# Attention and two MoE layers on one core: four small edits to buffers, banks and the place of one subtraction

## The chip, the cores and the metric

The program runs on one core of one Trainium2 chip. The metric is device time in microseconds (us) of one execution, as the median of several. Engines are named as in the profile: PE (TensorE, matmuls), DVE (VectorE), ACT (ScalarE), POOL (GpSimd), SP (SyncE, which only issues transfers here).

## The reference, cut to what matters

```
# 32 heads (4 batches x 8), 576 positions, head width 64, blocks of 64
scores = q @ k.T / 8, masked where block(query) < block(key)
attn   = exp(scores - max) / (sum + 1e-9)
x      = attn @ v                       # heads side by side: 2304 x 512
h1     = max(x @ w_in1, 0);   x2 = h1*h1 @ w_out1
h      = x2 @ w_in2                     # 2304 x 2048
P      = a0 + a1*h + a2*h^2 + a3*h^3;   Q = 1 + |b0||h| + |b1|h^2
out    = P / (Q + 1e-6) @ w_out2
```

## The kernel before, in words

**Three stages.** Until about 405 us the heads' attention runs, and the first half of the first MoE layer is woven into it (`moe_a`, six blocks of tokens, k = 0 to 5). Until 603 us the second half of that layer runs, and then the second layer, five blocks of tokens by 16 units u (hc, L780, is a unit's first product, yc, L898, its second). A scheduler places every instruction in its engine's queue when the program is built; each engine then runs its queue strictly in order and waits on semaphores. So an edit that adds a dependence, or takes one away, can reorder much that it does not name.

**High and low parts.** From head 10 (PLAIN) on each fp32 operand is split in a high part (float32r) and a remainder, the low part, and products are summed from three or four combinations. For head n, qh and kk are made one head ahead: ACT copies the high parts (L259, L260), DVE writes the low part of q into half of the tile q_two (L263; q_two and k_two exist twice and alternate over the heads), POOL writes the low part of k into the upper half of kk (L265), and SP copies kk's lower half into k_two (L266). PE's score products of head n (L335) read kk whole, so they wait for L265. The constant halves of q_two and k_two are filled once, by L231 and L232 in `make_two`.

**The other names.** p holds exponentials (ACT L371, normalised on POOL L399); tp is p transposed by PE (L300) in PSUM, which ACT (L441, high) and DVE (L443, low) move into pt (before head 10: pt_plain, L429); pv (L483) is p times v. ACT L486 and DVE L487 bring pv into xp, POOL L492 and L493 split xp into ring, the x that MoE reads. A tile of PSUM has a tag, and a tag has a number of banks ("mm" 2, "tp" 3); a product that takes a bank again waits for the readers of what was there. In `moe_a` ha (L540) goes to ACT (relu and square, L575 and L576) and DVE (L578, tile s), and POOL makes the low part (L579).

**The last stage's element work for unit u.** ACT: L878 |h| into ab, L880, L879 into wq; POOL squares (L881); DVE L882, L883 read h for the last time when r is not h's bank; then one unit later ACT Ln (L862) and Exp (L863, into r), DVE L864, L865, L866, all reading r; then ACT L857 and POOL L858 make g, which yc reads. ab has two buffers, h four banks: hc of u+4 needs the bank of u, and ab of u+2 the buffer of u.

Of the kernel before, what the change touches and what calls it, by code (L numbers as in the profile page):

```python
# [11 lines left out]
AF = mybir.ActivationFunctionType  # L12
ALU = mybir.AluOpType
# [4 lines left out]
P = 128  # L18
S = 576
SP = 640  # L20
D = 64
# [8 lines left out]
PLAIN = 10  # L30
# [14 lines left out]
def f(ap):  # L45
    return ap.bitcast(F32)
# [3 lines left out]
def attention_moe_moe(ctx: ExitStack, tc: tile.TileContext, q, k, v, wi1, wo1, wi2, wo2, a, b, out):  # L50
    nc = tc.nc
# [171 lines left out]
    q_two, k_two = [], []  # L223

    def make_two(un):
        early.release()
        late = tc.alloc_tile_pool(name="late", bufs=1, reuse_waits="tile")
        for n in range(2):
            q_two.append(late.tile([P, SP], F32R, name=f"q_two{n}"))
            k_two.append(late.tile([P, S], F32R, name=f"k_two{n}"))  # L230
            nc.scalar.activation(q_two[n][D:P], un.qr[D:P], AF.Copy)  # L231
            nc.scalar.activation(k_two[n][D:P], un.kr[D:P], AF.Copy)  # L232
        return late

    def load_v(un):
        src = v[un.hd].rearrange("p (c d) -> p c d", d=D)
# [12 lines left out]
    def prep_qk(un, step):  # L249
        if un.plain:  # L250
            if step == 0 and un.scale == 1.0:
                cols = un.qr[:, un.q0:un.q1]
                nc.gpsimd.tensor_scalar(cols, cols, SCALE, 0.0, op0=ALU.mult, op1=ALU.add)
            return
        if step == 0:
            hd = un.hd
            un.qh = attn.tile([P, SP], F32R, tag="qh", name=f"qh{hd}", bufs=2)
            un.kk = attn.tile([P, S], F32R, tag="kk", name=f"kk{hd}", bufs=2)
            nc.scalar.activation(un.qh, un.qr, AF.Copy, scale=SCALE)  # L259
            nc.scalar.activation(un.kk, un.kr, AF.Copy)  # L260
        else:
            un.q2, un.k2 = q_two[un.hd % 2], k_two[un.hd % 2]
            nc.vector.scalar_tensor_tensor(  # L263
                un.q2[0:D], un.qr[0:D], SCALE, f(un.qh[0:D]), op0=ALU.mult, op1=ALU.subtract)
            nc.gpsimd.tensor_tensor(un.kk[D:P], un.kr[D:P], f(un.kk[D:P]), op=ALU.subtract)  # L265
            nc.sync.dma_start(f(un.k2[0:D]), f(un.kk[0:D]))  # L266

    def prep_v(un, step):
# [20 lines left out]
    spsum, stats, gates, marks, spread = {}, {}, {}, [], {}  # L289
# [163 lines left out]
    def emit_pv(un, half):  # L453
# [4 lines left out]
        n = end - first  # L458
# [30 lines left out]
        if odd:  # L489
            at = S * (b_ % 2)  # L490
            xh, xl = (ring[:, z, hp, at + first:at + end] for z in range(2))
            nc.gpsimd.tensor_scalar(xh, xp[:, 0:n], 1.0, 0.0, op0=ALU.mult, op1=ALU.add)  # L492
            nc.gpsimd.tensor_tensor(xl, xp[:, 0:n], f(xh), op=ALU.subtract)  # L493
            nc.sync.dma_start(xs[:, hp, S * b_ + first:S * b_ + end], xp[:, 0:n])

    wA = {}
# [25 lines left out]
    def moe_a(k):  # L522
# [5 lines left out]
        def bank(nm):  # L528
            nonlocal count
            count += 1  # L530
            tag = "tp" if end_ and count % 2 else "mm"
            return ps1.tile([P, 512], F32, tag=tag, name=nm, bufs=BANKS[tag])

        gs = []
# [109 lines left out]
    for i in range(NI + 5):  # L644

        if i == FIRST:
            moes += [moe_a(0), moe_a(1)]
        elif i in (SECOND, SECOND + PER_B):
            moes.append(moe_a((i - MOE_AT) // PER_B))
        elif i == NI + 3:  # L650
            moes += [moe_a(4), moe_a(5)]
        if i < NI:
            emit_s(i)
        if 0 < i < 3:
            keep_busy(3, marks[-1])
        if 0 <= i - 1 < NI:
            emit_norm(i - 1)
        if i < NI:
            emit_max(i)
        gate = marks[-1 - AHEAD] if i < NI and i > AHEAD else None  # L660
        advance(steps(i + 0.5) - steps(i), gate)
        if i < NI:
            emit_exp(i)
        if 0 <= i - 4 < NI:
            un, gi = slots[i - 4]
            if gi % 2:
                emit_pv(un, gi // 2)
        if 0 <= i - 3 < NI:
            emit_t(i - 3)
        advance(steps(i + 1) - steps(i + 0.5), gate)  # L670
        if i == 4 * PLAIN - 4:
            late = make_two(slots[i][0])
        for back in range(4):
            n = units_at.get(i - back)
            if n is None:
                continue
            if back < 2 and n + 1 < len(units):
                prep_qk(units[n + 1], back)
                ahead = 4 if n + 4 < 2 * H else 2 if n + 2 >= 2 * H else 0
                if back == 1 and ahead and n + ahead < len(units):  # L680
                    load_qk(units[n + ahead])
            elif back >= 2:
                prep_v(units[n], back - 2)
                if back == 3 and n + 1 < len(units):
                    load_v(units[n + 1])
        if due(i) < due(i + 1):
            convA(*gates.values())
# [161 lines left out]
    for u in range(max(downs) + 1):  # L849
# [19 lines left out]
        if u < len(units):  # L869
# [11 lines left out]
            squared = (nc.vector if u >= len(units) - END else nc.gpsimd).tensor_tensor(w, w, ab, op=ALU.mult)  # L881
            nc.vector.tensor_tensor(t, h, t, op=ALU.mult)  # L882
            done = (taken, nc.vector.scalar_tensor_tensor(t, t, a1, h, op0=ALU.add, op1=ALU.mult))  # L883
            mid[u] = (ab, w, t, ab if u < LAG else h)
            if j + 1 < len(blocks3) and 3 <= m < 3 + 2 * KK and m % 2:
                with tc.issue_after(taken.ins), tc.issue_after(squared.ins):
                    split_x(xt[j + 1], m // 2 - 1, blocks3[j + 1][1])
# [81 lines left out]
```

## Time and profile before

| what | value |
|---|---|
| median of 3 runs | 1005.95 us (1005.1 to 1006.06) |
| the profiled execution | 1004.93 us, of which 1003.2 us span |
| PE busy | 992.0 us of the span |
| DVE, ACT, POOL busy | 724.8, 723.8, 570.5 us |
| mean granted TensorE clock | 1.000 |

PE's busy time is nearly the span, so what counts are the few places where PE waits, and what it waits for; the other engines' idle time counts only where it ends at such a place.

### The profile page before, as it was taken

The page shows a single profiled execution, that of the slowest core. Times are in us where ns is not written, and L with a number is a line of the kernel's source. Part 1 is how long each engine was busy: PE and PEld are TensorE (multiplying, and loading weights), DVE is VectorE, ACT ScalarE, POOL GpSimd, SP SyncE. Part 2 cuts the span into 40 slices and gives each one's busy share as a digit, 9 for nine tenths or more (in the row PEclk, how much of TensorE's full clock was granted, in tenths as well). Part 3 has the DMA queues.
Part 4 walks back from the last instruction along what each step waited for, and adds up shares of the span by engine and source line. Part 5 has one row for each costly group of instructions (what it writes and reads, how often), then busy time and mean ns, then how long its engine had stood idle before and what let it go on. Part 6 is the DMA issues. An engine that isn't in the chain of part 4 may idle for free.

```text
span 1003.2 us, 16323 instructions
## 1 busy us (share of the span) xinstructions
PE 992.0 (99%) x5361; PEld 864.6 (86%) x5361; DVE 724.8 (72%) x1389; ACT 723.8 (72%) x1590; POOL 570.5 (57%) x617
## 2 busy tenths in 40 slices
PE   8999999999999999999999999999999999999998
PEld 6678999888888899999888887888888888899997
DVE  7898687877787478767768766757666666666765
ACT  7888697887886467655455557867777777787885
POOL 5777597886787268421215386854655554555542
PEclk9999999999999999999999999999999999999999
DMA  9864334334332244569654651002001100200000
GB/s 295 267 198 149 114 113 132 89 106 130 105 107 83 97 131 124 207 184 300 230 191 151 231 157 58 1 1 84 1 1 32 42 1 1 74 1 1 32 1 32
DMA packets 63844, 106.67 MB, mean 106 GB/s; under 512 B 17040, under 2 KB 33424, under 8 KB 63760
## 3 DMA queue, kind: packets, MB, share of 16 engines
q1 hardware_dynamic: 63184, 105.05, 33.5%
q8 instruction: 42, 0.69, 0.3%
q10 hardware_dynamic: 576, 0.59, 0.2%
q14 instruction: 42, 0.34, 0.1%
HBM read 79.30 MB, written 23.07 MB: 102 GB/s over the span
## 4 chain that ended last, share of the span: by engine, by line
PE 91%; ACT 3%; DVE 2%; POOL 1%; DMA 1%; issue 1%; POOLq 0%; DVEq 0%; ACTq 0%; SPq 0%
PE yc L898 19%; PE hc L780 19%; PE hb L780 10%; PE yb L821 10%; PE ya L562 10%; PE ha L540 9%; PE tp L300 5%; PE pv L483 4%; PE sx L335 3%; PE sy L335 2%; PE pv L470 1%; DMA qr<-in_q_dram 1%; DMA raw_ai<-in_wi_dram 1%; POOL rb L387 0%; ACT p L371 0%
## 5 line engine op out<-in xcount | busy, mean ns | idle before, releaser
L780 PE MATMUL hc<-ring,w_ci 128*128 128x512 f32 (+1 forms) x960 | 210.2, 368 | 1.0 <-DVE t L866 1.0
L780 PEld LDWEIGHTS hc<-ring,w_ci 128*128 128x128 f32 x960 | 176.2, 188 | 27.0 <-DVE t L866 1.4
L898 PE MATMUL yc<-w_co,gc 128*128 128x512 f32 x792 | 191.7, 390 | 0.0
L898 PEld LDWEIGHTS yc<-w_co,gc 128*128 128x128 f32 x792 | 148.2, 188 | 29.3
L858 POOL TENSOR_TENSOR gc<-t,gc 128x512 fp32r<-128x512 f32 (+1 forms) x70 | 85.1, 1215 | 89.4 <-issue 61.0
L881 POOL TENSOR_TENSOR wq<-wq,ab 128x512 f32<-128x512 f32 (+1 forms) x78 | 92.8, 1190 | 75.0 <-ACT wq L879 74.7
L540 PE MATMUL ha<-ring,w_ai 128*128 128x512 f32 (+3 forms) x576 | 117.5, 348 | 0.5 <-DVE xp L487 0.5
L821 PE MATMUL yb<-gb,w_bo 128*128 128x512 f32 (+1 forms) x480 | 105.3, 367 | 0.0
L780 PE MATMUL hb<-ring,w_bi 128*128 128x512 f32 (+1 forms) x480 | 105.2, 367 | 0.0
L540 PEld LDWEIGHTS ha<-ring,w_ai 128*128 128x128 f32 x576 | 94.1, 189 | 11.3 <-issue 3.0
L715 POOL TENSOR_TENSOR ring<-ring 128x512 fp32r<-128x512 f32 (+1 forms) x40 | 52.4, 1311 | 88.0 <-ACT ring L714 83.2
L882 DVE TENSOR_TENSOR t<-hc,t 128x512 f32<-128x512 f32 (+1 forms) x80 | 50.9, 636 | 67.7 <-ACT t L880 67.7
L821 PEld LDWEIGHTS yb<-gb,w_bo 128*128 128x128 f32 x480 | 87.6, 188 | 11.4
L780 PEld LDWEIGHTS hb<-ring,w_bi 128*128 128x128 f32 x480 | 87.5, 188 | 11.1
L562 PE MATMUL ya<-gring,w_ao 128*128 128x352 f32 (+3 forms) x480 | 88.9, 331 | 0.0
L864 DVE SCALAR_TENSOR_TENSOR wq<-wq,hc 128x512 f32<-128x512 f32 (+1 forms) x78 | 49.3, 632 | 53.0 <-ACT hc L863 35.6
L300 PE MATMUL tp<-ident,p 128*128 128x128 f32 x480 | 82.1, 281 | 1.4 <-DVE stat L394 1.0
L562 PEld LDWEIGHTS ya<-gring,w_ao 128*128 128x128 f32 x480 | 75.9, 188 | 4.0 <-DVE s L578 0.2
L399 POOL TENSOR_SCALAR p<-p,stat 64x64 f32<-64x64 f32 (+4 forms) x110 | 60.3, 552 | 28.9 <-DVE stat L395 14.4
L443 DVE TENSOR_TENSOR pt<-tp,pt 128x128 fp32r<-128x128 f32 (+2 forms) x176 | 63.2, 391 | 18.6 <-ACT pt L441 11.9
L441 ACT ACTIVATE pt<-tp 128x128 fp32r<-128x128 f32 (+2 forms) x176 | 56.7, 365 | 19.3 <-PE tp L300 17.4
L878 ACT ACTIVATE ab<-hc 128x512 f32<-128x512 f32 (+1 forms) x80 | 44.2, 553 | 36.3 <-PE hc L780 36.0
(157 smaller groups left out, 2099.3 us busy)
## 6 DMA issues: line engine op xcount, KB each, us to landing
kr<-in_k_dram SPq DMA_DIRECT2D x32, 288.0 KB, 3.6
raw_ci<-in_wi_dram SPq DMA_DIRECT2D x16, 512.0 KB, 4.4
raw_co<-in_wo_dram SPq DMA_DIRECT2D x16, 512.0 KB, 4.0
qr<-in_q_dram SPq DMA_DIRECT2D x24, 320.0 KB, 3.2
ring<-xs SPq DMA_DIRECT2D x24, 256.0 KB, 4.2
raw_ai<-in_wi_dram SPq DMA_DIRECT2D x8, 512.0 KB, 5.2
raw_ao<-in_wo_dram SPq DMA_DIRECT2D x8, 512.0 KB, 4.6
raw_bi<-in_wi_dram SPq DMA_DIRECT2D x8, 512.0 KB, 3.9
```

Of the source, the lines that this page charges most:

```text
L300: yield nc.tensor.transpose(ps[:, P * n:P * (n + 1)], ptile(un, t)[:, P * c:P * (c + 1)], ident)
L399: nc.gpsimd.tensor_scalar(pv, pv, st[r:P, 6 + n:7 + n], 0.0, op0=ALU.mult, op1=ALU.add)
L441: nc.scalar.activation(high, src, AF.Copy)
L443: nc.vector.tensor_tensor(low, src, f(high), op=ALU.subtract)
L540: nc.tensor.matmul(ps[:, 0:n], w[:, zw, P * kk:P * (kk + 1)], ring[:, zx, kk, x0:x0 + n], start=i == 0, stop=i == 3 * KK - 1)
L562: nc.tensor.matmul(ps[c][:, 0:n], wA["o", m][:, zw, P * c:P * (c + 1)], gs[m][:, zg, 0:n], start=m == 0 and i == 0, stop=m == HALF - 1 and ...
L715: nc.gpsimd.tensor_tensor(lo, f(lo), f(hi), op=ALU.subtract)
L780: nc.tensor.matmul(ps[:, 0:n], w[:, zw, P * kk:P * (kk + 1)], xt[:, zx, kk, 0:n], start=i == 0, stop=i == 3 * KK - 1)
L821: nc.tensor.matmul(acc[j, c][:, 0:n], wB["o", m][:, zw, P * c:P * (c + 1)], g[:, zg, 0:n], start=m == 0 and i == 0, stop=last and i == 2)
L858: (nc.vector if u - 2 >= len(units) - END else nc.gpsimd).tensor_tensor(g[:, 1, 0:n], t, f(g[:, 0, 0:n]), op=ALU.subtract)
L881: squared = (nc.vector if u >= len(units) - END else nc.gpsimd).tensor_tensor(w, w, ab, op=ALU.mult)
L898: last = nc.tensor.matmul(acc[j, c], g[:, zg, P * c:P * (c + 1)], w3["o", m][:, zw, :], start=m == 0 and i == 0, stop=m == NM - 1 and i == 2)
```

## The change

Four edits. (1) The copies L231 and L232 for the second q_two and k_two are taken out of `make_two` and issued two slots later, behind that slot's exponentials. (2) L265, the low part of kk, may be placed only behind the latest L493. (3) In `moe_a` for k = 4 the first four products always take "mm" banks, where they took "tp" and "mm" in turn. (4) In the last stage r lies in ab (SBUF) for the units u = 0 to 3, where it did for 0 and 1; from then on it lies in h's bank (PSUM). Lines below 228 keep their numbers in the changed kernel; behind them the numbers are higher by 3, from the `with` in `prep_qk` by 4, and from the main loop's new call on by 7.

```diff
         for n in range(2):
             q_two.append(late.tile([P, SP], F32R, name=f"q_two{n}"))
             k_two.append(late.tile([P, S], F32R, name=f"k_two{n}"))
-            nc.scalar.activation(q_two[n][D:P], un.qr[D:P], AF.Copy)
-            nc.scalar.activation(k_two[n][D:P], un.kr[D:P], AF.Copy)
+        fill_two(un, 0)
         return late
+
+    def fill_two(un, n):
+        nc.scalar.activation(q_two[n][D:P], un.qr[D:P], AF.Copy)
+        nc.scalar.activation(k_two[n][D:P], un.kr[D:P], AF.Copy)
...
-            nc.gpsimd.tensor_tensor(un.kk[D:P], un.kr[D:P], f(un.kk[D:P]), op=ALU.subtract)
+            with tc.issue_after(spread["xl"].ins):
+                nc.gpsimd.tensor_tensor(un.kk[D:P], un.kr[D:P], f(un.kk[D:P]), op=ALU.subtract)
...
-            nc.gpsimd.tensor_tensor(xl, xp[:, 0:n], f(xh), op=ALU.subtract)
+            spread["xl"] = nc.gpsimd.tensor_tensor(xl, xp[:, 0:n], f(xh), op=ALU.subtract)
...
-            tag = "tp" if end_ and count % 2 else "mm"
+            tag = "tp" if end_ and count % 2 and (k > 4 or count > 4) else "mm"
...
+        if i == 4 * PLAIN - 2:
+            with tc.issue_after(gates["exp"].ins):
+                fill_two(slots[i][0], 1)
...
-            mid[u] = (ab, w, t, ab if u < LAG else h)
+            mid[u] = (ab, w, t, ab if u < 2 * LAG else h)
```

How the queues move, at the three places that the prediction speaks of. First DVE around the second q_two (the tile of head 11), before and then after; s0_5 frees a bank for the product ha0_7, and stat7 is a row maximum.

```order
L141 SCALAR_TENSOR_TENSOR cv_ao7_1208<-cv_ao7_1208,raw_ao7_1005 128x512
L578 SCALAR_TENSOR_TENSOR s0_5_1227<-ha0_5_1180,r0_5_1226 128x320
L358 TENSOR_REDUCE stat7_139<-sx39_1250 128x1
L431 COPY pt_plain_122<-tp36_0_1267 128x192
L431 COPY pt_plain_122<-tp36_0_1267 128x128
L358 TENSOR_REDUCE stat0_132<-sy40_1285 64x1
L358 TENSOR_REDUCE stat0_132<-sy40_1285 128x1
L263 SCALAR_TENSOR_TENSOR q_two1_1160<-qr19_1201,qh11_1320 64x640
```

```order
L141 SCALAR_TENSOR_TENSOR cv_ao7_1206<-cv_ao7_1206,raw_ao7_1005 128x512
L266 SCALAR_TENSOR_TENSOR q_two1_1158<-qr19_1199,qh11_1320 64x640
L582 SCALAR_TENSOR_TENSOR s0_5_1225<-ha0_5_1178,r0_5_1224 128x320
L362 TENSOR_REDUCE stat7_139<-sx39_1250 128x1
L435 COPY pt_plain_122<-tp36_0_1267 128x192
```

The low part of q for head 11 moves from behind the two maxima of slot 40 to ahead of s0_5. Second, POOL around kk21 and kk22 (the low parts of k for heads 21 and 22) and the split of xp18 (the pair of heads 18 and 19), before and then after.

```order
L265 TENSOR_TENSOR kk21_3008<-kr29_2900,kk21_3008 64x576
...
L579 TENSOR_TENSOR ga2_6_3048<-s2_6_3050,ga2_6_3048 128x512
L265 TENSOR_TENSOR kk22_3169<-kr30_3059,kk22_3169 64x576
L492 TENSOR_SCALAR ring_66<-xp18_0_2867 128x320
L493 TENSOR_TENSOR ring_66<-xp18_0_2867,ring_66 128x320
L399 TENSOR_SCALAR p3_1_99<-p3_1_99,stat2_134 128x448
```

```order
L583 TENSOR_TENSOR ga2_6_3048<-s2_6_3050,ga2_6_3048 128x512
L496 TENSOR_SCALAR ring_66<-xp18_0_2867 128x320
L497 TENSOR_TENSOR ring_66<-xp18_0_2867,ring_66 128x320
L269 TENSOR_TENSOR kk21_3008<-kr29_2900,kk21_3008 64x576
L403 TENSOR_SCALAR p3_1_99<-p3_1_99,stat2_134 128x448
L403 TENSOR_SCALAR p4_1_101<-p4_1_101,stat3_135 128x576
```

The subtraction for head 21 moves some ten instructions back, to right behind the split of xp18's first part, where the one for head 22 stood ahead of that split; the odd heads 13 to 31 all read like this, and the even heads' stands behind the second part's split. Third, ACT in the last stage from the Exp of unit 2 (units 2 to 5; wq is the denominator), before and then after.

```order
L863 ACTIVATE hc0_2_7443<-ab2_7456,cab_73 128x512
L878 ACTIVATE ab4_7550<-hc0_4_7537 128x512
L880 ACTIVATE t4_7552<-hc0_4_7537,coef_72 128x512
L772 ACTIVATE w_co13_7346<-w_co13_7346 128x512
L862 ACTIVATE ab3_7504<-wq3_7505,cab_73 128x512
L879 ACTIVATE wq4_7551<-ab4_7550,cab_73 128x512
L863 ACTIVATE hc0_3_7491<-ab3_7504,cab_73 128x512
L857 ACTIVATE gc2_7527<-t2_7458 128x512
```

```order
L870 ACTIVATE ab2_7456<-ab2_7456,cab_73 128x512
L869 ACTIVATE ab3_7504<-wq3_7505,cab_73 128x512
L870 ACTIVATE ab3_7504<-ab3_7504,cab_73 128x512
L864 ACTIVATE gc2_7527<-t2_7458 128x512
L885 ACTIVATE ab4_7550<-hc0_4_7537 128x512
L887 ACTIVATE t4_7552<-hc0_4_7537,coef_72 128x512
L779 ACTIVATE w_co13_7346<-w_co13_7346 128x512
L886 ACTIVATE wq4_7551<-ab4_7550,cab_73 128x512
L864 ACTIVATE gc3_7571<-t3_7506 128x512
```

The start of unit 4 (ab4, t4) moves from right behind the Exp of unit 2 to behind the Exp of unit 3 and gc2. On PE hc6 moves ahead of the end of yc1 and hc7 ahead of yc2, and hc8 stands behind all twelve products of yc3, where it stood behind eight.

## Rows read from the trace of the kernel before

**Rows 1.** The page: busy time, share of the span and instructions of each engine.

```profile
PE 992.0 (99%) x5361; PEld 864.6 (86%) x5361; DVE 724.8 (72%) x1389; ACT 723.8 (72%) x1590; POOL 570.5 (57%) x617
```

**Rows 2.** Timeline around 84 to 91 us: start, us, engine, line, tiles, idle time before.

```profile
84.55 2.04 DVE L263 SCALAR_TENSOR_TENSOR q_two<-qr,qh 64x640 fp32r<-64x640 f32 x1
84.68 0.66 PE L300 MATMUL tp<-ident,p 128*128 128x128 f32 x4 [0.30 <-ACT xp L478]
...
85.64 1.02 PE L335 MATMUL sy<-kr,qr 128*128 128x448 f32 x2 [0.30 <-ACT p L371]
...
90.48 0.48 DVE L578 SCALAR_TENSOR_TENSOR s<-ha,r 128x320 f32<-128x320 f32 x1
...
91.06 0.67 PE L540 MATMUL ha<-ring,w_ai 128*128 128x320 f32 x3
```

**Rows 3.** A group of ACT instructions by line: busy us, mean ns of one, idle before.

```profile
L231 ACT ACTIVATE q_two<-qr 64x640 fp32r<-64x640 f32 x2 | 1.5, 726 | 0.0
```

**Rows 4.** Timeline around 188.4 to 192.7 us.

```profile
188.54 1.43 POOL L265 TENSOR_TENSOR kk<-kr,kk 64x576 fp32r<-64x576 f32 x1 [0.96 <-ACT kk L260]
188.56 2.09 DVE L263 SCALAR_TENSOR_TENSOR q_two<-qr,qh 64x640 fp32r<-64x640 f32 x1
...
191.58 0.52 PE L300 MATMUL tp<-ident,p 128*128 128x128 f32 x3 [1.00 <-DVE stat L394]
...
192.52 0.31 PE L335 MATMUL sx<-kk,qh 128*128 128x320 f32 x1
```

**Rows 5.** Timeline around 211.4 to 214.9 us.

```profile
211.46 0.82 DVE L263 SCALAR_TENSOR_TENSOR q_two<-qr,qh 64x640 fp32r<-64x640 f32 x1
211.51 2.06 POOL L265 TENSOR_TENSOR kk<-kr,kk 64x576 fp32r<-64x576 f32 x1 [1.09 <-DVE xp L487]
...
213.66 0.46 POOL L492 TENSOR_SCALAR ring<-xp 128x320 fp32r<-128x320 f32 x1
...
214.20 0.88 POOL L493 TENSOR_TENSOR ring<-xp,ring 128x320 fp32r<-128x320 f32 x1
...
214.48 0.41 PE L335 MATMUL sx<-kk,qh 128*128 128x320 f32 x1
```

**Rows 6.** Timeline around 278 to 280 us.

```profile
278.18 1.88 POOL L265 TENSOR_TENSOR kk<-kr,kk 64x576 fp32r<-64x576 f32 x1
...
279.64 0.41 PE L335 MATMUL sx<-kk,qh 128*128 128x320 f32 x1
```

**Rows 7.** Timeline around 127.2 to 129 us.

```profile
127.30 0.81 DVE L263 SCALAR_TENSOR_TENSOR q_two<-qr,qh 64x640 fp32r<-64x640 f32 x1
...
128.00 0.93 PE L483 MATMUL pv<-pt,vs 128*128 128x128 f32 x6
...
128.10 0.26 DVE L443 TENSOR_TENSOR pt<-tp,pt 128x128 fp32r<-128x128 f32 x1
```

**Rows 8.** Timeline around 344.9 to 346.4 us, one PE row.

```profile
345.54 1.07 PE L540 MATMUL ha<-ring,w_ai 128*128 128x352 f32 x5 [0.48 <-DVE xp L487]
```

**Rows 9.** Timeline around 612 to 616.3 us.

```profile
612.26 1.00 DVE L864 SCALAR_TENSOR_TENSOR wq<-wq,ab 128x512 f32<-128x512 f32 x1 [1.20 <-ACT ab L863]
...
615.52 1.74 POOL L858 TENSOR_TENSOR gc<-t,gc 128x512 fp32r<-128x512 f32 x1 [2.80 <-ACT gc L857]
...
616.14 1.67 DVE L866 SCALAR_TENSOR_TENSOR t<-t,coef,ab 128x512 f32<-128x512 f32 x1
```

**Rows 10.** Timeline around 622.7 to 636.5 us, the last row PE's alone.

```profile
622.69 1.30 POOL L881 TENSOR_TENSOR wq<-wq,ab 128x512 f32<-128x512 f32 x1
622.75 0.60 ACT L878 ACTIVATE ab<-hc 128x512 f32<-128x512 f32 x1
...
624.75 0.74 DVE L866 SCALAR_TENSOR_TENSOR t<-t,coef,hc 128x512 f32<-128x512 f32 x1
...
625.54 0.72 PE L780 MATMUL hc<-ring,w_ci 128*128 128x512 f32 x2 [0.97 <-DVE t L866]
...
635.66 1.07 PE L780 MATMUL hc<-ring,w_ci 128*128 128x512 f32 x4
```

## The prediction, as it was written before the result

> **What bounds the kernel now.** I read the page first: PE is busy for 992.0 of 1003.2 us [rows 1], so all its idle time together is 11.2 us, and a change of buffers and order can only win back some part of that. Then I read PE's timeline for rows that carry an idle time and a releaser. Four such places belong to the four edits. At 84.68 and 85.64 PE waits twice, first for ACT L478 and then for ACT L371 [rows 2]. At 191.58 it waits for DVE [rows 4], at 345.54 for DVE L487 [rows 8], at 625.54 for DVE L866 [rows 10]. The last views are the timelines of the other engines at these places: what held the releaser, and what stands behind it. The reader should see that each wait comes from an engine that was doing something else at that moment. An edit that moves this something makes another thing late, and the price depends on what PE asks for next.
>
> All sums go against the profiled execution, 1004.93 us, of which 1003.2 are span; the median of the three runs is 1.0 higher, and I add the sum to the median.
>
> **Edit 1, two constant copies later: 0.0 us (-0.9 to +0.4).** Four copies of about 0.7 us each [rows 3] stand on ACT in front of the work that PE waits for at 84.68. Two of them go, 1.4 us, which is more than both waits: their rows show 0.30 idle each, and as the matmuls before them overlap it is more from start to start, 0.57 and 0.58 us where 0.11 is usual, 0.93 lost in all. The copies themselves come back behind the exponentials of a later slot, and nothing reads them for some time, so their new place costs nothing directly. But look at what is late next. The product ha that starts at 91.06 takes a bank that DVE L578 releases; L578 runs from 90.48 to 90.96, so PE starts 0.10 us behind it and has no slack there [rows 2]. With 0.93 us won, PE asks at 90.13. In the changed order the low part of q for head 11 stands on DVE between L141 and this L578. It costs 0.82 us alone [rows 5] and up to 2.09 beside POOL [rows 4]. On the other side DVE is itself earlier: the L263 of head 10 took 2.04 at 84.55 [rows 2] beside L265, which edit 2 moves away, so up to 1.2 us comes back. L578 then ends between 90.96 - 1.2 + 0.8 = 90.6 and about 91.4, where PE wants it at 90.13. So 0.5 to 1.3 of the 0.93 is given back: about nothing is left. The low end is the case that the DVE wait does not come.
>
> **Edit 2, kk's low part behind x's split: +1.9 us (-1.2 to +2.5).** It removes the largest wait. At 188.54 POOL starts L265 and DVE L263 starts 0.02 later; L263 takes 2.09 instead of 0.82 and ends 0.68 behind L265's end [rows 4]. At 211.46 the order of starts is the other way round, and there L265 takes 2.06 and ends 1.29 behind L263's end [rows 5]. So these two exclude each other, and the second to start is held almost whole. DVE's queue behind L263 is late, and PE's row at 191.58 shows 1.00 idle; from start to start it is 1.16. This goes: -1.16.
>
> What it adds is a tight chain for the odd heads, whose L265 used to run a head earlier. Now it stands behind L492 and L493, and these wait for DVE L487. For head 21: L487 ends at 211.43, L263 follows on DVE at 211.46 for 0.82 [rows 5]. L492 comes to POOL at about the same moment, is held until 212.28 and ends about 0.35 later, at 212.65. L493 takes 0.88, and L265 at least 1.43 [rows 4, 5]; with 0.08 between them the end is 212.65 + 0.08 + 0.88 + 0.08 + 1.43 = 215.1. PE's sx of head 21 wants kk at 214.48 [rows 5]: 0.65 late. If L492 is the first of the two, the end is 214.43 and nothing is late; since L263 needs no signal from another engine and L492 does, I take the held case at three quarters, 0.5. Head 29 has the same spacing: 0.5. Head 19 too: its chain starts at 188.53, 22.90 us earlier, and ends at 215.1 - 22.90 = 192.2; its sx stands at 192.52, but that is 191.36 once the wait of 1.16 is gone [rows 4]: 0.9 held, 0.0 free, taken as 0.5. Head 27 can be read directly, since an L265 already stands behind L493 there: it ends at 278.18 + 1.88 = 280.06, and sx wants kk at 279.64 [rows 6]: 0.45. Head 17 looks like 27, but PE's order gives it some 0.4 us more: 0.3. Head 13 is of another kind: its L265 comes straight behind L493 and starts at about 127.13, ahead of DVE's L263 at 127.30, so L263 ends as in rows 4 at 127.13 + 1.43 + 0.68 = 129.2 instead of 128.11. L443 behind it ends at 129.6, where it ended at 128.36, and the last products of the pv group, which had begun by 128.70, read its result [rows 7]: 0.8. The other odd heads and all the even ones have 0.7 us or more to spare. The sum is 0.8 + 0.3 + 0.5 + 0.5 + 0.45 + 0.5 = 3.05, less 1.16: +1.9. Every collision lost would give 3.65 - 1.16 = +2.5, none lost -1.16.
>
> **Edit 3, banks of the last block: 0.0 us (-0.1 to +0.3).** ha of block 4 no longer needs the bank that L487 frees at 345.48 [rows 8]. But the next instruction behind the transposes is now the second pv of head 31, which takes this same bank. The wait of 0.75 from start to start changes its owner.
>
> **Edit 4, r of units 2 and 3 in SBUF: +0.7 us (-1.2 to +1.2).** hc6 takes unit 2's bank, which now comes free with L883 of unit 2, before 622, instead of L866 at 625.49 [rows 10]. PE's 1.24 us at 625.54 (two starts, 1.13 and 0.11 over the usual pace) goes. But r now holds the ab buffer for three more DVE instructions, and ab4 needs the buffer of unit 2. ab4 started at 622.75, without waiting for any of this [rows 10]; now it must wait for L866 of unit 2. That L866 is also later, because its chain now has two operands in SBUF. Units 0 and 1 show the price: L864 took 1.00 and L866 1.67 where 0.69 and 0.74 are usual, and a POOL instruction beside it took 1.74 instead of 1.30 [rows 9, 10]. The L864 of unit 2 at 622.8 meets the POOL row at 622.69, which runs to 623.99 [rows 10], so L864 ends at about 624.5, L865 at 625.3, L866 at 626.0 if nothing else holds it and at 627.0 if L866 is held as in rows 9. With gc2 ahead of it ab4 starts at 626.6 to 627.6, some 4 to 5 us later than before. From ab4 to unit 4's Exp there are then twelve ACT instructions of 0.58 to 0.81 us, 7.1 us without a wait, and three of DVE, 2.2: L866 of unit 4 ends at 636.0 to 637.0. hc8 needs its bank. hc8 started at 635.66 [rows 10]; it is 1.24 earlier by the wait that is gone and 0.9 later by four more products of yc3 ahead of it, so PE wants it at 635.3. The new wait is 0.7 to 1.7 us by this, and more where gc3 on the way waits for L866 of unit 3. I take 1.9: +0.7 net. The best case is that the old wait goes and none comes, -1.2.
>
> The rows show one of three DVE instructions held in each of units 0 and 1 [rows 9]. The Trainium skill, in "SBUF — State Buffer", section "Who interferes with whom", says that a DVE instruction with two SBUF inputs contends with any GpSimd instruction that reads SBUF, and that whoever is first has the shared pair for its whole length. By the rows alone edit 4 comes to about +0.3; by the rule, with POOL busy without a gap from 618 on, all six DVE instructions of units 2 and 3 could be held, and it comes to +1.2. My +0.7 stands between.
>
> **The sum.** 0.0 + 1.9 + 0.0 + 0.7 = +2.6: 1007.5 for a profiled execution, 1008.6 against the median. The bounds add up to -3.4 and +4.4.
>
> **The rivals.** (a) My forecast: the waits are exchanged for later ones that are together longer; 1008.6, and 1008.0 to 1010.4 where most collisions are lost. (b) They are exchanged evenly: POOL's L492 wins the port from L263, so that heads 19, 21 and 29 cost nothing (-1.5), and hc8 waits only 0.7 (-1.2). For it speaks that the margins are some tenths, against it that L263 already stood ahead in two of the three rows in question. Sum -0.1: 1005.9. (c) Faster, by one mechanism: L265 ends before PE's next sx at each odd head, and DVE's L263 never meets it. That decides itself at the head-21 chain: its end must lie before 214.48 instead of at 215.1. Then edit 2 gives its 1.16 whole, DVE is earlier around 90 us as well, so that 0.5 of edit 1 stays, and with hc8 at 0.7 wait (-0.5): 1003.8. Against it stands head 27, where L265 in its new place is already seen to end 0.4 behind PE's need [rows 6]. (d) That an edit does nothing holds only for the third.
>
> **How the numbers follow.** A measurement of this kernel can tell about 0.2%, 2.0 us, from no change. I give (a) 0.6, (b) 0.25, (c) 0.15. Of (a) a tenth lies under +2.0, and (b) all but wholly within; (c) at -2.2 lies on the lower edge, four fifths of it beyond. So: slower 0.54, same 0.34, faster 0.12. The range of (a) alone is 1007.0 to 1010.4; with (b) taken in, and the best part of (c) left out, 1004.4 to 1010.8.
>
> **What would show it.** In the changed profile: no idle time for ACT L478 and L371 near 84, but a PE row of ha near 91 that waits for DVE's L578. No row like 191.58; instead sx rows of odd heads that wait for POOL's L265, and a pv row near 129 that waits for DVE L443. At 345 the same idle time before pv. At 625 no wait, and one at hc8 for DVE L866, with DVE's L864 to L866 of units 2 and 3 over 1 us. I am wrong if the sx rows of heads 19, 21, 27 and 29 show no releaser on POOL, or if hc8 waits for less than 1.2 us.

## The result, and the profile after

The changed kernel takes 1011.66 us (median of 6, 1011.59 to 1013.51) where the kernel before, beside it on the same chip, takes 1006.0 (median of 6, 1004.75 to 1007.33). The ratio is 1.0062, with an interval of 1.0049 to 1.0075: slower by 5.7 us, where 2.6 was forecast. The direction was right and the size was not, and the time lies 0.9 above the range. The profiled execution took 1013.51 us with a span of 1011.4. Three far slower executions are left out of all that follows: one of the first kernel without heads 17, 18 and 26 (5630 us, with its profile) and two of the kernel before (1639 and 1397 us).

In the changed file the lines are shifted: by 3 behind line 228, by 4 from `prep_qk` on, by 7 from the main loop on. So L263 and L265 are now L266 and L269, L492 and L493 are L496 and L497, and L864 to L866 are L871 to L873.

The page has PE busy 3 us longer than in [rows 1], DVE nearly 5:

```profile
PE 995.0 (98%) x5361; PEld 865.5 (86%) x5361; DVE 729.6 (72%) x1389; ACT 723.4 (72%) x1590; POOL 569.8 (56%) x617
```

PE's waits in the changed kernel, by line and releaser: us in total, times, the longest. (The rows left out lie before 24 us, in code that the change does not touch.)

```profile
PE hc L787 <- DVE t L873: 2.4, 1, 2.4
PE sx L339 <- POOL kk L269: 1.9, 4, 0.5
...
PE ha L544 <- DVE s L582: 1.2, 1, 1.2
...
PE pv L487 <- ACT pt L445: 1.0, 3, 0.5
...
PE pv L487 <- DVE stat L398: 0.7, 1, 0.7
PE pv L487 <- DVE xp L491: 0.6, 1, 0.6
```

And the rows of PE's timeline on which these stand:

```profile
92.06 1.73 PE L544 MATMUL ha<-ring,w_ai 128*128 128x320 f32 x10 [1.17 <-DVE s L582]
...
130.40 0.33 PE L487 MATMUL pv<-pt,vs 128*128 128x128 f32 x1 [0.69 <-DVE stat L398]
...
182.55 0.85 PE L487 MATMUL pv<-pt,vs 128*128 128x128 f32 x5 [0.48 <-ACT pt L445]
...
194.87 0.41 PE L339 MATMUL sx<-kk,qh 128*128 128x320 f32 x1 [0.45 <-POOL kk L269]
...
217.50 0.42 PE L339 MATMUL sx<-kk,qh 128*128 128x320 f32 x1 [0.50 <-POOL kk L269]
...
271.62 0.61 PE L487 MATMUL pv<-pt,vs 128*128 128x128 f32 x3 [0.24 <-ACT pt L445]
...
283.92 0.41 PE L339 MATMUL sx<-kk,qh 128*128 128x320 f32 x1 [0.44 <-POOL kk L269]
...
306.63 0.41 PE L339 MATMUL sx<-kk,qh 128*128 128x320 f32 x1 [0.51 <-POOL kk L269]
...
350.55 0.47 PE L487 MATMUL pv<-pt,vs 128*128 128x256 f32 x2 [0.57 <-DVE xp L491]
...
643.09 4.61 PE L787 MATMUL hc<-ring,w_ci 128*128 128x512 f32 x12 [2.39 <-DVE t L873]
```

The waits of [rows 2, 4] for ACT L478, L371 and DVE L394 are gone, and so is that of hc6 in [rows 10]. In their places stand ha near 91, a pv near 129, four sx that wait for POOL, and hc8, all of them forecast; and two pv that wait for ACT's copy into pt, 0.48 at 182.55 (0.29 before) and 0.24 at 271.62 (none before), which were not. (The third of that line, 0.24 near 328, the kernel before has too.)

One thing more is in no list of waits. These are windows of the changed kernel around the wait of 2.39 us: the stretch, its length, then busy time and instructions of PE, PE's weight loads, DVE, ACT and POOL, the granted clock, the DMA share and GB/s.

```profile
641.00:643.80 2.80, 0.71 (x3) 0.63 (x4) 2.65 (x5) 2.80 (x5) 2.80 (x3) 1.00 0.00 0
643.80:647.30 3.50, 3.50 (x11) 2.68 (x9) 2.13 (x3) 3.29 (x7) 3.21 (x4) 0.51 0.02 5
```

PE was busy for 0.71 of 2.80 us, and behind that the granted clock is 0.51, TensorE's lower level of 1.2 GHz, for 3.5 us. PE did the work of 3.50 x 0.51 = 1.8 us there, so 1.7 us are lost to the clock. The kernel before has 1.00 throughout. The executions of the changed kernel fall in two kinds by it: the two with a mean clock of 0.998 or less took 1013.51 and 1013.06, the four others 1011.6 to 1011.7.

Where the time went is read by taking one and the same instruction of PE in both traces (the first product of a given sy or hc) and subtracting its starts. This execution is 0.86 late by 73 us already, in code that the change doesn't touch (0.44 in another profile of the same kernel), so I count from there. "Edit 2" is the trace of edit 2 alone, below.

| stretch, us of before | what stands there | forecast | after | edit 2 alone |
|---|---|---|---|---|
| 73 to 108 | edit 1, and edit 2 near 85 to 92 | 0.0 | 0.0 | +0.68 |
| 108 to 149 | head 13 | +0.8 | +1.35 | +1.36 |
| 149 to 175 | head 17 | +0.3 | -0.15 | -0.15 |
| 175 to 198 | wait at 191.58 gone, head 19 | -0.66 | +0.36 | +0.33 |
| 198 to 215 | head 21 | +0.5 | +0.59 | +0.59 |
| 215 to 258 | | 0 | +0.09 | +0.14 |
| 258 to 269 | | 0 | +0.60 | +0.65 |
| 269 to 280 | head 27 | +0.45 | +0.59 | +0.59 |
| 280 to 307 | head 29 | +0.5 | +0.62 | +0.62 |
| 307 to 616 | edit 3 | 0.0 | +0.33 | +0.01 |
| 616 to 677 | edit 4 | +0.7 | +3.05 | -0.03 |
| sum | | +2.6 | +7.4 | +4.8 |

7.4 less the 1.7 of the clock is 5.7, the difference of the medians (most of the six executions have no such fall, and the profiled one has it).

### The profile page after: what moved, and what is told of

It reads as the page before. It is cut to its first block, busy times and chain, and to the rows that moved or that the text cites. A ratio compares the mean times of both kernels' runs of the same rounds, so it can differ in the third digit from the quotient of the medians.

```text
span 1011.4 us, 16312 instructions
## 1 busy us (share of the span) xinstructions
PE 995.0 (98%) x5361; PEld 865.5 (86%) x5361; DVE 729.6 (72%) x1389; ACT 723.4 (72%) x1590; POOL 569.8 (56%) x617
## 4 chain that ended last, share of the span: by engine, by line
PE 86%; ACT 5%; DVE 4%; POOL 3%; issue 1%; DMA 1%; SPq 0%; POOLq 0%; ACTq 0%; DVEq 0%
PE yc L905 18%; PE hc L787 18%; PE yb L828 10%; PE hb L787 10%; PE ya L566 9%; PE ha L544 8%; PE tp L304 4%; PE pv L487 3%; PE sx L339 2%; PE sy L339 2%; PE pv L474 1%; DMA qr<-in_q_dram 1%; DVE stat L362 1%; POOL kk L269 1%; ACT p L375 1%
## 5 line engine op out<-in xcount | busy, mean ns | idle before, releaser
L865 POOL TENSOR_TENSOR gc<-t,gc 128x512 fp32r<-128x512 f32 (+1 forms) x70 | 85.4, 1219 | 92.6 <-issue 61.2
L889 DVE TENSOR_TENSOR t<-hc,t 128x512 f32<-128x512 f32 (+1 forms) x80 | 50.9, 637 | 67.8 <-ACT t L887 67.8
L871 DVE SCALAR_TENSOR_TENSOR wq<-wq,hc 128x512 f32<-128x512 f32 (+1 forms) x76 | 47.9, 631 | 51.4 <-ACT hc L870 35.4
L447 DVE TENSOR_TENSOR pt<-tp,pt 128x128 fp32r<-128x128 f32 (+2 forms) x176 | 63.2, 391 | 18.1 <-ACT pt L445 11.1
```

Of the source, the lines that this page charges most:

```text
L447: nc.vector.tensor_tensor(low, src, f(high), op=ALU.subtract)
L865: (nc.vector if u - 2 >= len(units) - END else nc.gpsimd).tensor_tensor(g[:, 1, 0:n], t, f(g[:, 0, 0:n]), op=ALU.subtract)
```

## The experiments

My theory of the result: each wait was exchanged for a later one, as forecast, and the sum came out too small because edit 2 made other work late than the two engines that I had followed, and because edit 4's wait costs clock as well. The rivals: edits 1 and 3 are not free; the difference is that of executions; or the half clock is general and has nothing to do with edit 4. All times are medians against the kernel before on the same chip, with the ratio's interval in brackets.

### Edits apart: all but 2, 2 alone, 4 alone, 1 alone

The diffs are the pieces of the change above. Edit 2 alone is

```
+            with tc.issue_after(spread["xl"].ins):
                 nc.gpsimd.tensor_tensor(un.kk[D:P], un.kr[D:P], f(un.kk[D:P]), op=ALU.subtract)
```

with `spread["xl"]` set at x's low part; edit 4 alone is `ab if u < 2 * LAG else h`; edit 1 alone is the two functions around `fill_two`.

Edits 1, 3 and 4, without 2:

> Edits 1, 3 and 4 without edit 2 (the low part of k is placed freely, as before). Theory A, that two things cost the time (edit 2 makes low parts of k and q late in the attention, edit 4 makes unit 4's ab wait): only edit 4's share is left, +1.2 us where the granted clock stays full and up to +3.0 where it halves for some us behind the new wait at hc8; 1007 to 1009 us. The waits of sx rows for POOL's kk are gone and the one of 1.0 us near 191 is back. Rival B, that edits 1 and 3 cost through the order that they leave: +4 us or more remains. Rival C, that edit 2 is harmless and the wait at hc8 with the clock behind it is all: +5.7 us remains.

Edit 2 alone:

> Edit 2 alone. Theory A: +4 us (3 to 5), 1010 us, with four sx rows (heads 19, 21, 27, 29) that wait about 0.5 us each for POOL's kk, and a pv row near 129 us that waits 0.7 us for DVE; no loss of clock, since no wait is as long as 2 us. Rival B: below +2 us. Rival C: 0 us.

Edit 4 alone:

> Edit 4 alone. Theory A: no wait at hc6, one of about 2.4 us at hc8 for DVE's last instruction of unit 4, net +1.2 us with the clock at 1.00 throughout and +2.9 us where it halves; 1007 to 1009 us. Rival C: +5 us. If the exchange were even, as my least favourable reading of the rows had it not: 0 us.

Edit 1 alone:

> Edit 1 alone. Theory A, as the prediction had it: the two waits at 84 us go and come back as one for DVE's s at the product ha near 91 us; 0.0 us (-0.9 to +0.4). Rival H, that this new wait comes only with edit 2: -0.9 us.

Stage C is the second layer, from 603 us of the kernel before on.

| edits | median, us | ratio | from the trace |
|---|---|---|---|
| 1, 3, 4 | 1008.05 | 1.0024 [1.0015, 1.0032] | hc8 waits 2.4; stage C +1.39 at clock 1.00 |
| 2 | 1010.65 | 1.0048 [1.0036, 1.006] | four sx waits, two pv waits for ACT; +4.8 from 73 us to the end, 4.1 of it from 108 us on |
| 4 | 1008.06 | 1.0024 [1.0015, 1.0033] | hc8 waits 2.4; stage C +1.40 at clock 1.00 |
| 1 | 1005.09 | 0.9995 [0.9987, 1.0004] | -0.4 near 85 to 94; ha waits 0.50 for DVE s L581 |

So edit 2 carries most of the loss, and edit 4 the rest. Edit 1 is within what a measurement can tell, with the wait at ha that was forecast. Without edit 2 the wait at 191.58 is back, as 1.0 for DVE in PE's waits. Edit 4 alone costs 1.4 us by its waits in both profiles, which have a clock of 1.00; its median is 2.5 above before, and 7 of its 11 timed executions have a mean clock of 0.998 or less (7 of 12 for edits 1, 3 and 4), where the kernel before has 1 of 28. So the medians do not add: 2 alone and 1, 3, 4 together are 5.1 + 2.5 = 7.6 above before, where the whole change is 5.7 above. By the traces without the clock, from 73 us on, they are 4.8 + 1.7 = 6.5 against 5.7; 0.3 of what is left lies between 73 and 108 us, where edit 1's gain and edit 2's loss meet, and 0.35 in the stretch of edit 3.

### Edit 2: which heads, and behind what

kk's low part behind x's high part (L492) in place of its low part, `tc.issue_after(spread["xh"].ins)`; edit 2 with `if un.hd % 2 == 0 else ExitStack()`, for the even heads alone; and with `if un.hd % 2`, for the odd ones alone:

> Edit 2 alone in another form: the low part of k is held behind the high part of x (the first of POOL's two instructions for x) and not behind the low part, so it comes one instruction of 0.9 us earlier. Theory A says that the waits of about 0.5 us are a margin missed by a few tenths: all four sx waits go, the wait near 191 does not come back, and the time is 1 to 2.5 us below before: 1003.5 to 1005. Rival D, that what costs is the collision of POOL and DVE at their shared port wherever the subtraction stands behind x: +2 us or more, as with edit 2.

> Edit 2 for the even heads alone (the low part of k of heads 10, 12 ... 30 waits for x's split; the odd heads' is placed freely). Theory A, that edit 2's loss sits in the odd heads, which have the least time between x's split and PE's score product: no sx row waits for POOL's kk, no wait near 129 us for the low part of head 13; the time lies between -1 and +1 us of before. Theory E, that the loss comes from the order that the dependence leaves on POOL and DVE as a whole, whichever heads carry it: +2 us, half of edit 2's.

> Edit 2 for the odd heads alone. Theory A: nearly all of edit 2's loss and none of its gain, +4 to +5 us, with the wait of 1.0 us near 191 back. Theory E: +2 us.

Behind the high part: 1005.70, 1.0001 [0.9992, 1.001]. Even heads: 1006.15, 1.0006 [0.9997, 1.0015]. Odd heads: 1013.76, 1.0080 [1.0067, 1.0093].

In the first two no sx waits for POOL, so the tight chain of the odd heads is what makes those waits. But neither gains anything, and the 1 to 2.5 us that I expected of the first did not come. Behind the high part 0.56 is won between 186 and 198 us and 0.57 lost between 269 and 280, where a pv waits 0.23 for DVE. With the even heads alone 0.92 is won near 190; 0.67 is lost between 73 and 108 and 0.62 between 258 and 269, where pv waits 0.24 for ACT's copy into pt, as in the whole edit. So these two losses belong to the even heads, to which I had given slack. The loss at the pv of head 16, between 175 and 186, does not come with the even heads alone (0.0 there).

The odd heads alone are worse than the whole edit. The low part of the even heads then runs ahead of that of the odd ones, and two sy wait 1.4 us each for POOL. Here is one of them in PE's timeline of that kernel:

```profile
219.07 0.30 PE L336 MATMUL sy<-kk,qh 128*128 128x64 f32 x1 [1.42 <-POOL kk L266]
```

And the windows behind it:

```profile
219.00:219.50 0.50, 0.42 (x4) 0.43 (x4) 0.43 (x1) 0.00 (x0) 0.40 (x2) 1.00 0.00 0
219.50:222.90 3.40, 3.40 (x11) 2.82 (x11) 0.58 (x2) 0.91 (x4) 3.40 (x6) 0.51 0.50 125
222.90:230.00 7.10, 7.10 (x44) 6.24 (x42) 5.01 (x15) 4.57 (x12) 2.41 (x5) 1.00 0.08 25
```

The clock is halved here too, in a kernel without edit 4, so the half clock does not belong to edit 4's code. It stands behind a long wait, but not behind each: at the other wait of 1.42 us, at 310.10 in the same trace, the clock stays at 1.00.

### Edit 2: ACT's queue at heads 16 and 24

In the trace of edit 2 alone ACT's timeline in front of the pv at 182 reads:

```profile
178.94 0.60 ACT L576 ACTIVATE r<-ha 128x512 f32<-128x512 f32 x1 [0.18 <-PE ha L541]
179.44 0.73 ACT L259 ACTIVATE qh<-qr 128x640 fp32r<-128x640 f32 x1
180.06 0.67 ACT L260 ACTIVATE kk<-kr 128x576 fp32r<-128x576 f32 x1
180.64 0.62 ACT L577 ACTIVATE gring<-r 128x512 fp32r<-128x512 f32 x1
181.16 0.58 ACT L576 ACTIVATE r<-ha 128x512 f32<-128x512 f32 x1
181.64 0.27 ACT L442 ACTIVATE pt<-tp 128x128 fp32r<-128x128 f32 x1
```

and in the kernel before:

```profile
177.90 0.61 ACT L575 ACTIVATE r<-ha 128x512 f32<-128x512 f32 x1
178.54 0.63 ACT L576 ACTIVATE gring<-r 128x512 fp32r<-128x512 f32 x1
179.07 0.58 ACT L575 ACTIVATE r<-ha 128x512 f32<-128x512 f32 x1
179.55 0.27 ACT L441 ACTIVATE pt<-tp 128x128 fp32r<-128x128 f32 x1
```

In the kernel before, the copies of the next heads' q and k (qh, kk) are already done there, and r, gring, r run straight in front of the copy into pt. The order of the program on ACT is made anew when kk's low part moves: the two copies now stand behind the first r, 1.2 us from start to start, with PE's pv behind them. At head 24 gring and a second r come in front of the copy into pt, which they followed before. Two ways to take this away. Edit 2 without heads 17, 18 and 26, which leaves ACT's order at both places as it was:

```
+            with tc.issue_after(spread["xl"].ins) if un.hd not in (17, 18, 26) else ExitStack():
```

> Edit 2 for all heads but 17, 18 and 26: with these three left as before, ACT's queue at heads 16 and 24 has the scaled q and the copy of k of the next head but two in front of the copies into pt again, as in the kernel before, while heads 13, 19, 21, 27 and 29 keep the new order. Theory: 1.2 of edit 2's 4.1 us came from those copies being late (the two pv waits for ACT near 182 and 271). Then both waits are gone, the waits of sx for POOL at heads 19, 21, 27 and 29 stay at about 0.5 each, and the time is about 2.9 us above before (1.5 to 3.5). Rival: the two steps at 182 and 271 come from POOL or DVE being late in another way; then they stay and the time is about 4 above before, as with edit 2 whole.

> Edit 2 for all heads but 17, 18 and 26, once more, since the profile of the first run fell on a disturbed execution: the times came out at 1.004 of before where 1.0015 to 1.0035 was expected. Theory: the two pv waits for ACT near 182 and 271 are gone in the profile, and a new collision at one of the three heads put back (their low part of kk in its old place meets DVE's work on q of the head before) costs about 1 us. Rival: the pv waits are still there, though ACT's order is that of before; then ACT's queue was not their cause.

And edit 2 whole, with the second r tied behind the copy into pt:

```
+                copied[i] = nc.scalar.activation(high, src, AF.Copy)
...
+        with tc.issue_after(copied[i - 4].ins) if i in (71, 103) else ExitStack():
             advance(steps(i + 1) - steps(i + 0.5), gate)
```

> Edit 2 for all heads, and ACT's relu (r of unit 1) at heads 16 and 24 tied behind the copy into pt that the products of pv wait for at 182 and 271; the relu takes 0.5 of ACT's time there. Theory: 1.2 of edit 2's 4.1 us is that ACT has work in front of these two copies that it did not have there before. Then both pv waits for ACT fall from 0.48 and 0.24 to nothing or nearly, and at heads 19 and 27, whose sx the tie also puts later in PE's order, the waits for POOL get smaller: 1.5 to 3 us above before. Rival: the two steps are due to DVE or POOL; then pv waits there for DVE instead and the time is about 4 above before.

Without the three heads: 1009.78, 1.0040 [1.0027, 1.0054], and in the second run 1008.68, 1.0035 [1.0023, 1.0048]. Tied: 1008.77, 1.0038 [1.0025, 1.005]. The pv in the tied kernel's timeline stand without an idle time:

```profile
182.04 0.92 PE L485 MATMUL pv<-pt,vs 128*128 128x128 f32 x6
...
270.67 0.91 PE L485 MATMUL pv<-pt,vs 128*128 128x128 f32 x6
```

From 108 us to the end the traces show +2.6 without the three heads and +3.0 tied, where the whole edit 2 has +4.1: less by 1.5 and 1.1, forecast 1.2. The pv wait for ACT at 271 is gone in both; that at 182 is gone with the tie, and without the three heads it is 0.29, as in the kernel before. So ACT's queue was the cause of what edit 2 added at these two places, shown in the traces. The times came out high: 4.2 and 3.3 above before without the three heads (1.5 to 3.5 expected), 3.4 tied (1.5 to 3 expected). I had left out the 0.7 between 73 and 108 us, which both traces have. The times cannot by themselves tell 1.1 us apart: the intervals are wider. No new collision came, which I had offered as the reason between the two runs. The tie also did not shorten the sx waits of heads 19 and 27, 0.49 each in its trace; that part was wrong.

### Edit 4: is it the buffer, the held DVE, or the size of the wait

r of units 2 and 3 in a buffer of its own, so that ab4 needs no release, `ab if u < LAG else tmp("o", n, f"r{u}") if u < 2 * LAG else h`; and r of unit 2 alone in ab, `ab if u < LAG + 1 else h`:

> Edit 4 alone, but r of units 2 and 3 lies in an SBUF tile of its own (the tag o, which is free in the last stage) and not in ab. The DVE instructions still read two operands from SBUF, but ab is free as early as before. Theory F, that the wait of 2.4 us at hc8 comes from ab being held: it goes, ab4 starts near 623 again, the granted clock stays at 1.00 in nearly all executions, and what is left is what the shared port costs, a wait of 0 to 1.8 us at yc3: -1.2 to +0.7 us against before. Rival G, that the slower DVE instructions at the shared port make the wait: hc8 still waits 2 us or more, +1.2 us and more.

> Half a dose of edit 4, alone: r of unit 2 in the ab buffer, r of unit 3 in its PSUM bank as before. Theory: the wait of hc6 (1.24 from start to start) goes, the ab buffer of unit 3 is free early and only that of unit 2 late, so the wait of hc8 is about 0.7 and yc may wait 0.4 for gc2: 0 to 0.5 us above before by the waits, and the granted clock stays at 1.0 in most executions, since no wait is longer than 1 us. Rival: the buffer of unit 2 alone decides; then hc8 waits 2.4 as with the full edit, +1.4 by the waits and the half clock in most executions, 2.4 above before.

With its own buffer: 1007.78, 1.0022 [1.0011, 1.0034], 2.4 above before where theory F allowed 0.7 at most. ab4 starts at 622.62, the wait of hc8 is gone, and the next products take its place, in PE's timeline of that kernel:

```profile
634.53 2.11 PE L898 MATMUL yc<-w_co,gc 128*128 128x512 f32 x8 [1.93 <-ACT gc L857]
```

So the ab buffer makes the wait of hc8, but it is not the whole matter. DVE's instructions with two operands in SBUF are held beside POOL with or without it (four of the six took 1.18 to 1.68 here), and if ab4 doesn't wait for them, the products of units 2 and 3 do. Part of that is ACT's queue: t of unit 3 is written at 632.26, and its g starts on ACT at 633.86, behind work of other units. Stage C is 0.95 longer at clock 1.00, and 8 of 12 timed executions have a mean clock of 0.998 or less.

With r of unit 2 alone: 1006.21, 1.0008 [0.9999, 1.0017]. Its waits:

```profile
PE hc L780 <- DVE t L866: 0.6, 1, 0.6
...
PE yc L898 <- ACT gc L857: 0.4, 1, 0.4
```

0.7 and 0.4 were expected. Stage C is +0.44, and 1 of 11 executions has a mean clock of 0.998, where the kernel before has 2 of 15 beside it. The dose decides, and with the smaller waits the clock stays in nearly all executions.

### The changed kernel once more

No edit.

> The changed kernel as it is, for more executions. Theory: two kinds of executions, by whether the granted clock falls to a half behind the wait of 2.4 us at hc8: about 5.6 us above before where the mean clock is 1.0, and 7 to 7.5 above where it is 0.997 or 0.998. In the profile, the time from that wait to the end of the stage is longer by 1.3 than before without the fall, by 3.0 with it. Rival: the executions differ for another reason (the start, the DMA), and the mean clock does not go with the time.

1011.38, 1.0059 [1.0045, 1.0072]. Two executions with a mean clock of 0.997 took 1012.83 and 1012.91, the three others 1010.87 to 1011.38: 1.4 to 2.0 us apart, where the window gives 1.7. In the profile, one of the former, stage C is 3.04 longer than before.

### Two versions from these

Edit 1, and edit 2 for head 20 alone, the one head whose low part of kk meets L263 at 188.54 [rows 4] and makes PE wait; and the same with the split of the next block's x in the last stage two units later:

```
+            with tc.issue_after(spread["xl"].ins) if un.hd == 20 else ExitStack():
...
-            if j + 1 < len(blocks3) and 3 <= m < 3 + 2 * KK and m % 2:
+            if j + 1 < len(blocks3) and 5 <= m < 5 + 2 * KK and m % 2:
```

> Edit 1, and edit 2 for head 20 alone. The kernel before loses 1.16 us at the one place (191.6) where the low part of kk of head 20 holds DVE's instruction on q of head 19 for 2.09 us; with this one instruction behind the split of x, no odd head gets a tight chain. Theory: the wait of 1.0 goes and nothing takes its place at heads 13, 19, 21, 27 and 29; with edit 1's 0 to 0.4 the kernel is 0.5 to 1.5 us faster than before. Rival: as with the two variants of edit 2 that lost no wait of sx and still gained nothing, a later wait of DVE or ACT takes the 1.1 us back; then within 0.3 of before.

> As the kernel with edit 1 and head 20 alone, and in the last stage the split of the next block's x starts two units later (m from 5 on instead of from 3 on), so that POOL is free of it while DVE works on units 0 and 1 and less of L864 and L866 there is held. Theory: the wait of hc6 for DVE (1.24 us from start to start) falls to about 0.5; 1 to 2 us faster than before. Rival: the split is then finished too late for the next block, whose products wait near 750 us for POOL, 1 to 2 us; then no gain or a loss of about 1.

The first: 1004.46, 0.9989 [0.998, 0.9997]. The second: 1004.17, 0.9988 [0.9979, 0.9996]. Both are faster than the kernel before, by 1.1 and by 1.2 to 1.4 us, a gain that the intervals just tell from none; they do not tell the two from each other. In the trace of the first, head 20 brings 0.77 and edit 1 0.39; in that of the second stage C is shorter by 0.5. DVE's timeline of the first has the instruction on q alone, 0.82 where [rows 4] have 2.09:

```profile
188.65 0.82 DVE L266 SCALAR_TENSOR_TENSOR q_two<-qr,qh 64x640 fp32r<-64x640 f32 x1
```

and the transposes behind it in PE's timeline wait for nothing:

```profile
190.51 0.49 PE L304 MATMUL tp<-ident,p 128*128 128x128 f32 x3
```

In the second hc6 waits less than half of [rows 10]:

```profile
624.11 3.06 PE L787 MATMUL hc<-ring,w_ci 128*128 128x512 f32 x12 [0.44 <-DVE t L873]
```

The wait near 750 us that the rival expected did not come. Of the 1.16 us at 191.58 all is won at the transposes and 0.77 is kept. The other 0.39 goes in PE's next three steps, from the transposes to pv (0.48 where it was 0.27), to sx (0.73, was 0.67) and to the second sx (0.25, was 0.14), in which PE shows no wait; what makes them longer is open.

## Why the prediction was right in direction and wrong in size

**Edit 1, 0.0 forecast.** Right, with its reason. Alone it wins 0.4 and meets DVE at ha; in the changed kernel ha waits 1.17 and starts at 92.06, which less the 0.86 is 0.14 behind [rows 2], and the stretch comes out even. That it is quite even is partly luck: the forecast had edit 2 bring DVE forward here by up to 1.2 us, and in the traces edit 2 takes back the 0.4 that edit 1 keeps alone.

**Edit 2, +1.9 forecast, +4.8 alone (+4.1 beside edit 1).** The chains of POOL and DVE came as worked out. For heads 13 and 19, and for units 2 to 4 further on, the other engines' timeline of the changed kernel:

```profile
127.99 1.42 POOL L269 TENSOR_TENSOR kk<-kr,kk 64x576 fp32r<-64x576 f32 x1
128.16 1.93 DVE L266 SCALAR_TENSOR_TENSOR q_two<-qr,qh 64x640 fp32r<-64x640 f32 x1
...
130.09 0.26 DVE L447 TENSOR_TENSOR pt<-tp,pt 128x128 fp32r<-128x128 f32 x1
...
191.22 0.82 DVE L266 SCALAR_TENSOR_TENSOR q_two<-qr,qh 64x640 fp32r<-64x640 f32 x1
191.28 1.08 POOL L496 TENSOR_SCALAR ring<-xp 128x320 fp32r<-128x320 f32 x1 [1.05 <-DVE xp L491]
192.44 0.88 POOL L497 TENSOR_TENSOR ring<-xp,ring 128x320 fp32r<-128x320 f32 x1
193.40 1.42 POOL L269 TENSOR_TENSOR kk<-kr,kk 64x576 fp32r<-64x576 f32 x1
...
628.08 1.68 DVE L871 SCALAR_TENSOR_TENSOR wq<-wq,ab 128x512 f32<-128x512 f32 x1 [1.71 <-ACT ab L870]
629.16 1.75 POOL L722 TENSOR_TENSOR ring<-ring 128x512 fp32r<-128x512 f32 x1
629.80 1.66 DVE L872 SCALAR_TENSOR_TENSOR ab<-wq,ab 128x512 f32<-128x512 f32 x1
631.50 0.75 DVE L873 SCALAR_TENSOR_TENSOR t<-t,coef,ab 128x512 f32<-128x512 f32 x1
632.17 0.69 DVE L871 SCALAR_TENSOR_TENSOR wq<-wq,ab 128x512 f32<-128x512 f32 x1
632.89 0.69 DVE L872 SCALAR_TENSOR_TENSOR ab<-wq,ab 128x512 f32<-128x512 f32 x1
633.00 1.74 POOL L865 TENSOR_TENSOR gc<-t,gc 128x512 fp32r<-128x512 f32 x1 [2.08 <-ACT gc L864]
633.62 1.68 DVE L873 SCALAR_TENSOR_TENSOR t<-t,coef,ab 128x512 f32<-128x512 f32 x1
...
641.69 0.68 DVE L889 TENSOR_TENSOR t<-hc,t 128x512 f32<-128x512 f32 x1
642.29 0.74 DVE L873 SCALAR_TENSOR_TENSOR t<-t,coef,hc 128x512 f32<-128x512 f32 x1
```

At head 13 L269 starts at 127.99, which less 0.86 is the 127.13 of the forecast. L447, the old L443, ends at 130.35 and the pv that reads pt starts at 130.40; the list of waits names DVE's L398, which came last before it. At head 19 L496 is held to 192.36 behind DVE's 0.82, and the chain ends at 193.40 + 1.42 = 194.82; less the 2.66 that the trace is late there, that is 192.16, forecast 192.2. The four sx waits are 0.44 to 0.51, each costing about 0.6 where 0.45 to 0.5 was taken. The rival (c), that the chains end in time, is refuted by these rows, and so is the even exchange (b).

The step that failed is "The other odd heads and all the even ones have 0.7 us or more to spare", which put every other effect of edit 2 at nothing. As to kk it may hold: no sx of another head waits for it. But in the trace of edit 2 alone 1.9 of the missing 2.9 us lie in places that this sentence gave nothing: 0.68 between 73 and 108 us; 0.57 at the pv of head 16, between 175 and 186; and 0.65 at that of head 24. I had looked at POOL's and DVE's margins only. The two pv waits come from ACT, whose queue the program ordered anew, and the even heads alone already show the loss at 258 to 269 us. Of the 0.68, 0.26 is there at the ha of 90.93, which waits 0.22 for DVE's s; the rest shows no wait. In the changed kernel, where edit 1 evens out the first of these, the two pv are 1.2 of the 2.2 us by which edit 2 exceeds its forecast. What remains is in the terms. Head 13 is 1.35 where 0.8 was taken: its sy behind the pv starts 1.18 later than before, as the wait stands in the middle of a group and what overlapped before no longer does. Head 17's 0.3 did not come. Of the gain of 1.16 at 191.58 only part is kept even without any chain, 0.77 with head 20 alone. Two of the recorded sums are slightly off: the collisions, all lost, are 3.75 and not 3.65, and the upper end of the range, 1010.8, is 0.4 above what the bounds give; neither changes the outcome.

**Edit 3, 0.0 forecast.** The wait changed its owner as forecast, 0.57 at 350.55 where [rows 8] have 0.48. But 0.3 is lost between about 395 and 426 us, 0.7 with edits 1, 3 and 4, in stretches where PE shows no wait; the kernels without edit 3 lose nothing there. No run has edit 3 alone, so the cause is open.

**Edit 4, +0.7 forecast, +1.35 by its waits and up to 1.7 more by the clock.** The mechanism is as worked out, and its size was too small. Less the 5.24 us that the trace is late at the start of the stage, ab4 starts at 627.6, the late end of my 626.6 to 627.6, and hc8 is wanted at 635.46, forecast 635.3. L873 of unit 4 ends at 637.8, forecast 636.0 to 637.0: ACT's twelve instructions took 7.4 where 7.1 was taken, and another unit's L889 stands in front of it on DVE, from 641.69 to 642.37, which I had not counted. So the wait is 2.39 where 1.9 was taken. The Trainium skill, in "SBUF — State Buffer", section "Who interferes with whom", has the engine that comes first to the shared pair keep it for its whole instruction. The trace agrees in kind: three of the six DVE instructions of units 2 and 3 took 1.66 to 1.68, the others 0.69 to 0.75. Its reading at full strength, that all six are held, rested on POOL being busy without a gap, and that did not come: POOL was idle for 2.08 us, from 630.91 to 633.00. Two of the three DVE instructions at the usual pace (631.50 and 632.17) had no POOL instruction beside them; the third (632.89) began 0.11 ahead of POOL's L865, which then took 1.74 where 1.30 is usual. So the rows agree with the rule, and my value between the two readings had too short a queue behind it.

The clock was not in the forecast at all. With it, edit 4's median is +2.5 alone. It is not what the median of the changed kernel missed, since four of its six executions have no such fall.

## What to carry to other kernels

An edit that ties one instruction behind another moves the order on engines that it doesn't name; before giving a slack to "all the others", compare the order of every engine that PE waits for, not only of the two that the edit is about. Where an edit removes one collision, apply it to the one place that has it: in the traces head 20 alone gains 0.8 us where all heads lose 4.8. And a wait on PE is not priced by its length alone: the clock behind it has to be read as well.

## What the runs showed of the chip that I had not expected

Behind a wait of PE of 2.39 us, and behind one of 1.42, the granted clock was half, 0.51, for about 3.4 us; that costs 1.7 us, more than the shorter wait itself. It does not come each time: the profiles of edit 4 alone and of edits 1, 3 and 4 have the wait of 2.4 us and a clock of 1.00 behind it. Over all runs, kernels with a wait of 1.4 to 2.4 us had a mean clock of 0.998 or less in 30 of 50 timed executions. The kernel before had it in 8 of the 92 beside them, and the changed ones without such a wait in 7 of 85, so it is rarer without such a wait, but not absent. What in an execution decides it, these runs do not show.
